# Batch 0 of a Fourier mixing kernel: load order, folds, and the E row of its first four steps

## The chip, the cores and the metric

The kernel runs on one core of a Trainium2 chip. The metric is device time in microseconds (us) of one launch. One run before the change was also recorded by the hardware profiler; all times of single instructions come from that run.

## The reference

`x` has 8 batches of 3008 rows and 256 columns. Each batch goes through a two-dimensional Fourier transform of which the real part is kept; the result, 24064 rows of 256, goes through a gated layer with d_ff = 1536.

```python
X = np.fft.fft(x, axis=1)          # along the 3008 rows
X = np.fft.fft(X, axis=2)          # along the 256 columns
x = X.real.astype(np.float32).reshape(B * S, D)
gate = 1.0 / (1.0 + np.exp(-(x @ w_gate)))
val = x @ w_val
return (gate * val @ w_out).astype(np.float32)
```

The three weights come from a float32 array multiplied by a numpy scalar, and reach the kernel as float64.

## The kernel before, in words

**The algebra.** The transform along the columns is linear, so it is merged into the weights: `merge` multiplies a block of 256 columns of w_gate or w_val by a small column table (`dt`) on TensorE and keeps two forms, G1 and G2. The transform along the rows is a multiplication by cosine and sine tables, made small by symmetry: rows s, 3008 - s, 1504 + s and 1504 - s are added and subtracted first (the folds), so that 126 partitions times 6 rows remain, and even and odd frequencies are summed apart. Each batch has three results over its 1505 frequencies: pk (cosine sums of the even column part, 128 partitions), qk (sine sums of the odd part, 128 partitions), and ek, the cosine sums of column 128 alone. ek is a single row of 1505 numbers; it is needed on all 128 partitions, since line 447 multiplies it by a scalar of each partition (`ge`, row 0 of G2 turned into a column by a small DMA).

**The main loop.** A step (`front`, `gate`, `back`) handles 256 frequencies and 128 columns of d_ff, for gate and value at once: TensorE makes pa = G1 · pk and pb = G2 · qk, VectorE makes ae = ek * ge + pa (line 447, twice), then z = ae + pb and ae - pb (lines 450 and 451), ScalarE takes the sigmoid, VectorE multiplies gate by value (line 462), GpSimd prepares differences, and TensorE multiplies by w_out (`back`). 12 steps make a chunk of 256 frequencies, 6 chunks a batch, 8 batches the kernel. PSUM for pa, pb and merges is a ring of four banks (`bank`); `po0` to `po3` are four more.

**The order is written by hand.** Each engine runs its instructions in program order. A dictionary `side` holds work to be issued at the end of a given step, `pre` work to be issued before the sigmoid of a step. SP issues nearly all DMAs, in program order; ScalarE's queue issues a few.

**The weights.** There are 18 blocks (`jobs`): gate c, value c and output c for c = 0 to 5. A float64 block is 512 KB. `weight_load` fetches it as pairs of int32; `weight_parts` is two ScalarE instructions (lines 221 and 222), `weight_join` three on VectorE (lines 231, 232, 234) and one addition on GpSimd (line 236). `weight_use` then merges the block (gate, value) or arranges it (`forms`, output). `weight_round` does parts and join of several blocks. Lines 252 and 253 copy G2 and G1 out of PSUM on ScalarE, line 255 issues the ge DMAs. In steps 0 to 8 the loop still prepares blocks 9 to 17.

**Batch 0 before the loop.** SP loads gate 0 and value 0, then x (two halves, line 116), the cosine table (two halves, line 159), four more blocks, the sine table, and four more. Gate 0 and value 0 are prepared and merged first. `fold_ops(0, 3)` folds x on VectorE with a share on GpSimd. TensorE makes the sums of pk and of ek (`cos`), each with 12 matmuls of 376 or 377 columns, ek with column 128 repeated 128 times as the stationary operand so that it comes out on all partitions; then the sine sums (`sin`). `places` (lines 370 and 373) puts sums and differences of even and odd parts into pk, qk, ek. For batches 1 to 7, `e_sums` makes ek of all seven at once, as rows of seven, stores them to DRAM (`ed`), and `seq_start` reads one row back to 128 partitions.

Of the kernel before, what the change touches and what calls it, by code (L numbers as in the profile page):

```python
# [7 lines left out]
F32 = mybir.dt.float32  # L8
# [43 lines left out]
def kernel(  # L52
# [101 lines left out]
    tr = dram.tile([P, 2, NQ, NE + NO], F32, name="tr")  # L154
    ed = dram.tile([B - 1, NK], F32, name="ed")

    def load_table(t, nq):
        for q in range(0, NQ, nq):
            nc.sync.dma_start(out=ST[0][0:NP, t, q : q + nq], in_=stab[:, t, q : q + nq])

# [15 lines left out]
    shared = {}  # L176
    KEEP = 10

    def weight_load(j):


        w, c = jobs[j]
        src = (moe_w_gate, moe_w_val, moe_w_out)[w]
        src = src[2 * c * P : 2 * (c + 1) * P, :] if w == 2 else src[:, c * WC : (c + 1) * WC]
        src = src.rearrange("(c p) f -> p c f", p=P)

        def some(n, pool, tag):

            key = tag, (j - 6) // 3 if tag == "c7" else 0
            if key not in shared:  # L190
                shared[key] = pool.tile([P, n, 2 * WC], F32, name=f"w{tag}", tag=tag)
            return shared[key]

        if j < KEEP:
            pool, tag = ((zp, "z"), (pqp, ("pk", "qk", "ek")[j % 3]), (op, "os"), (sp, "sf"))[
                j // 3 if j < 6 else j // 2 - 1]
            raw = pool.tile([P, 2, WC, 2], I32, name="raw", tag=tag)
            if j < 6:
                pool, tag = ((app, "ae"), (hp, "h"))[j // 3]
                ws = pool.tile([P, 2, WC], F32, name="ws", tag=tag)  # L200
            else:
                ws = some(3, cp, "c7")[:, (j - 6) % 3].rearrange("p (c f) -> p c f", c=2)
        else:
            both = some(12, xp, "x4")
            r, i = (j - KEEP) % 3 * 2, 6 + (j - KEEP) % 6
            raw = both[:, r : r + 2].rearrange("p a n -> p (a n)").bitcast(I32).rearrange(
                "p (c f w) -> p c f w", c=2, w=2)
            ws = both[:, i].rearrange("p (c f) -> p c f", c=2)
        WS[j] = ws
        if src.dtype == F32:  # L210
            nc.sync.dma_start(out=ws, in_=src)
        else:
            RAW[j] = raw
            nc.sync.dma_start(out=raw.rearrange("p c f w -> p c (f w)"), in_=src.bitcast(I32))

    def weight_parts(j):

        if j in RAW:
            raw, ws = RAW[j], WS[j]
            lo, hi = raw[:, :, :, 0], raw[:, :, :, 1]  # L220
            nc.scalar.activation(ws, hi.bitcast(F32), AF.Abs)
            nc.scalar.activation(lo, lo.bitcast(U32), AF.Copy, scale=2.0 ** -29)
# [22 lines left out]
    def merge(ws, g, c, other):  # L245
        cs = slice(c * WC, (c + 1) * WC)
        ps = bank("ps", other)
        for h in range(2):
            for t in range(2):
                mm(ps[:, h * WC : (h + 1) * WC], dt[:, t, h * HD : (h + 1) * HD], ws[:, t, :],  # L250
                   h == 0 and t == 0, t == 1)
        nc.scalar.copy(G2[:, g, cs], ps[:, WC : 2 * WC])
        nc.scalar.copy(G1[:, g, cs], ps[:, 0:WC])
        for f in range(c * WC // P, (c + 1) * WC // P):
            (nc.sync if c else nc.scalar).dma_start(
                out=ge[:, g, f : f + 1], in_=G2[0:1, g, f * P : (f + 1) * P])
# [16 lines left out]
    def fold_ops(b, nq):  # L273
# [18 lines left out]
        def across(e, blk, q):  # L292
            e.tensor_tensor(x4[:, 1 - blk, q], x4[:, 0, q], x4[:, 2, q],
                            op=(ALU.add, ALU.subtract)[blk])
# [19 lines left out]
        else:  # L314

            def half1(q):
                point(nc.vector, 2, 3, q)
                first(nc.vector, 2, 3, q)
                for blk in range(2):
                    across(nc.vector, blk, q)  # L320
                    feat(nc.vector, *parts[blk], q)

            def half2(q):
                across(nc.vector, 0, q)
                feat(nc.vector, *parts[0], q)
                across(pool, 1, q)
                feat(pool, *parts[1], q)
            for q in qs:
                point(nc.vector, 0, 1, q)
            first(nc.vector, 0, 1, slice(0, NQ))  # L330
            point(pool, 2, 3, qs[1])
            first(pool, 2, 3, qs[1])
            ops += [lambda: half1(qs[0]), lambda: half2(qs[1])]
        for blk, (v, r) in enumerate(parts):
            W[b, blk] = (v[:, :, 0:HD], r[:, :, 0:HD],
                         v[:, :, HD : HD + 1].to_broadcast([v.shape[0], NQ, P]))
        return ops
# [43 lines left out]
    def seq_start(b):  # L381
# [3 lines left out]
        if b:  # L385
            nc.sync.dma_start(out=PQE[b][2], in_=ed[b - 1 : b, :].to_broadcast([P, NK]))

# [13 lines left out]

    def e_sums():


        ps = bank("pe")
        m = B - 1
        at_ = lambda blk, par: slice((2 * blk + par) * TB, (2 * blk + par) * TB + m)
        for q in range(0, NQ, 2):
            for blk in range(2):
                c0, n = ((0, NE), (NE, NO))[blk]  # L410
                for par in range(2):
                    mm(ps[at_(blk, par), 0:n], x8[:, :, 1 + 2 * blk, q + par],
                       ST[0][0:NP, 0, q + par, c0 : c0 + n], q == 0, q == NQ - 2)
        er = cp.tile([P, NK], F32, name="er", tag="c7")[0:m]
        a = evp.tile([P, NE], F32, name="a", tag="a")[0:m]
        e1 = evp.tile([P, NE], F32, name="a", tag="a")[0:m]
        nc.scalar.copy(a, ps[at_(0, 1), 0:NE])
        nc.scalar.copy(e1[:, 0:NO], ps[at_(1, 0), 0:NO])

        def rest():  # L420
            places(er, 0, True, a, ps[at_(0, 0), 0:NE])
            nc.scalar.copy(a[:, 0:NO], ps[at_(1, 1), 0:NO])
            places(er, 1, False, e1[:, 0:NO], a[:, 0:NO])
            nc.scalar.dma_start(out=ed, in_=er)
        return rest

# [5 lines left out]
    def front(p, fh):  # L432
# [6 lines left out]
        pa = bank("pa").rearrange("p (g n) -> p g n", g=2)[:, :, 0:n]  # L439
        pb = bank("pb").rearrange("p (g n) -> p g n", g=2)[:, :, 0:n]  # L440
        for g in range(2):
            mm(pa[:, g], G1[:, g, fs], pk[:, ks], g == 0, True)
        for g in range(2):
            mm(pb[:, g], G2[:, g, fs], qk[:, ks], g == 0, True)
        ae = app.tile([P, 2, CH], F32, name="ae", tag="ae")[:, :, 0:n]
        for g in range(2):
            nc.vector.scalar_tensor_tensor(out=ae[:, g], in0=ek[:, ks], scalar=ge[:, g, f : f + 1],  # L447
                                           in1=pa[:, g], op0=ALU.mult, op1=ALU.add)
        z = zp.tile([P, 2, 2, CH], F32, name="z", tag="z")[:, :, :, 0:n]
# [116 lines left out]
    nc.gpsimd.memset(zero, 0.0)  # L566
    nc.scalar.dma_start(out=dt, in_=dtab.rearrange("(c p) d -> p c d", p=P))
    for j in range(2):
        weight_load(j)
    load_x(0)  # L570
    load_table(0, NQ // 2)
    for j in range(2, 6):
        weight_load(j)
    load_table(1, NQ)
    for j in range(6, KEEP):
        weight_load(j)

    def weight_round(*js):
        for j in js:
            weight_parts(j)  # L580
            weight_join(j)

    weight_parts(0)
    weight_parts(1)
    weight_join(0)
    weight_join(1)
    weight_use(0)
    weight_use(1)
    seq_start(0)
    cos = [seq_group(0, blk, what, (2 * blk, 2 * blk + 1) if what else None)  # L590
           for blk in range(2) for what in (0, 2)]
    for i, f in enumerate(fold_ops(0, NQ // 2)):
        f()
        for sums, _, _ in cos:
            sums(*range(i * NQ // 2, (i + 1) * NQ // 2))
    sin = [seq_group(0, blk, 1) for blk in range(2)]
    for sums, _, _ in sin:
        sums(*range(NQ))
    evacuate = [then for _, then, _ in cos + sin]
    for then, js in zip(evacuate, ((2, 3, 4), (5,), (), (), (6, 7), (8,))):  # L600
        weight_round(*js)
        then()()
    for j in range(KEEP, KEEP + 3):
        weight_load(j)
    weight_use(2)

# [12 lines left out]
    pre = {}  # L619
    for j in range(9, len(jobs)):  # L620
        pre.setdefault(j - 9, []).append(lambda j=j: weight_parts(j))
        at(j - 9, lambda j=j: weight_join(j))
        if KEEP <= j < len(jobs) - 3:
            at(j - 9, lambda j=j: weight_load(j + 3))
    for j in range(3, len(jobs)):
        w, c = jobs[j]
        at(2 * c + (-3, -2, 1)[w], lambda j=j: weight_use(j))

# [12 lines left out]
    at(3 * i0, e_fold)  # L641
    split(3 * i0 + 3, e_sums)
    at(3 * i0 + 5, table_again)
# [91 lines left out]
```

## Time and profile before

| | |
|---|---|
| three runs | 1992.41, 1993.08, 1996.01 us; median 1993.08 |
| profiled execution | span 1992.2 us, mean granted TensorE clock 0.996 |
| x halves have landed, by the waits of line 280 | 11.29 and 16.33 us |
| folds on VectorE end, last sine sum on TensorE ends | 26.7 and 49.7 us |
| first step starts (first pa matmul) | 51.24 us |
| the step with the last weight block ends | about 98 us |

The page gives busy time of each engine over the whole span; the timeline gives the instructions of one engine in order of time, with the idle time before each and what ended it. PE is TensorE, DVE VectorE, ACT ScalarE, POOL GpSimd, SP the engine that issues DMAs. Numbers after L are lines of the kernel. A float32 matmul stands as two records.

### The profile page before, as it was taken

The page shows a single profiled execution, that of the slowest core. Times are in us where ns is not written, and L with a number is a line of the kernel's source. Part 1 is how long each engine was busy: PE and PEld are TensorE (multiplying, and loading weights), DVE is VectorE, ACT ScalarE, POOL GpSimd, SP SyncE. Part 2 cuts the span into 40 slices and gives each one's busy share as a digit, 9 for nine tenths or more (in the row PEclk, how much of TensorE's full clock was granted, in tenths as well). Part 3 has the DMA queues.
Part 4 walks back from the last instruction along what each step waited for, and adds up shares of the span by engine and source line. Part 5 has one row for each costly group of instructions (what it writes and reads, how often), then busy time and mean ns, then how long its engine had stood idle before and what let it go on. Part 6 is the DMA issues. An engine that isn't in the chain of part 4 may idle for free.

```text
span 1992.2 us, 28166 instructions
## 1 busy us (share of the span) xinstructions
PE 1965.1 (99%) x9504; PEld 1737.3 (87%) x9504; DVE 1777.8 (89%) x3221; ACT 497.2 (25%) x876; POOL 1348.3 (68%) x1704
## 2 busy tenths in 40 slices
PE   6999999999999999999999999999999999999998
PEld 4888889888988889888898888988899888998888
DVE  7999979978999789997999979999799988898887
ACT  3422222222222222222222222222222222222221
POOL 3678867865787467874678646886478854655655
PEclk8999999999999999999999999999999999999999
DMA  7262421112020201202011020111200000000001
GB/s 265 85 134 77 154 90 48 48 27 75 16 66 25 82 19 23 73 11 90 17 44 46 17 90 17 43 47 32 75 11 12 21 27 11 11 20 12 11 17 26
DMA packets 160815, 100.33 MB, mean 50 GB/s; under 512 B 128419, under 2 KB 151715, under 8 KB 157994
## 3 DMA queue, kind: packets, MB, share of 16 engines
q1 hardware_dynamic: 158850, 98.00, 17.0%
q8 instruction: 76, 1.25, 0.3%
q10 hardware_dynamic: 1822, 0.54, 0.1%
q14 instruction: 67, 0.55, 0.1%
HBM read 73.74 MB, written 50.17 MB: 62 GB/s over the span
## 4 chain that ended last, share of the span: by engine, by line
PE 96%; DMA 2%; DVE 1%; ACT 0%; issue 0%; POOL 0%; SPq 0%; ACTq 0%; DVEq 0%; POOLq 0%
PE po L100 43%; PE pa L100 24%; PE pb L100 24%; PE ev L100 4%; DMA ge<-G 1%; DMA st<-in_stab_dram 1%; PE od L100 1%; PE ps L100 0%; DMA raw<-in_moe_w_val_dram 0%; DVE ae L447 0%; POOL wx L236 0%; PE pe L100 0%; DVE z L451 0%; DVE wx L232 0%; DVE os L509 0%
## 5 line engine op out<-in xcount | busy, mean ns | idle before, releaser
L672 ACT ACTIVATE z<-z 128x512 f32<-128x512 f32 (+1 forms) x576 | 358.5, 622 | 1297.5 <-DVE z L451 1297.5
L100 PE MATMUL pb<-qk,G 128*128 128x256 f32 (+1 forms) x2304 | 581.8, 375 | 2.5 <-DVE ae L447 2.5
L100 PE MATMUL pa<-pk,G 128*128 128x256 f32 (+1 forms) x2304 | 582.1, 375 | 0.0
L447 DVE SCALAR_TENSOR_TENSOR ae<-ek,ge,pa 128x256 f32<-128x256 f32 (+1 forms) x1152 | 488.1, 464 | 68.5 <-PE pa L100 65.0
L100 PE MATMUL po<-sf,wf 128*128 128x256 f32 (+1 forms) x2304 | 534.6, 375 | 0.0
L466 POOL TENSOR_TENSOR sf<-h 128x256 f32<-128x256 f32 (+1 forms) x288 | 206.9, 718 | 448.7 <-DVE h L462 448.7
L100 PEld LDWEIGHTS pb<-qk,G 128*128 128x128 f32 x2304 | 437.3, 190 | 53.6 <-DVE ae L447 4.0
L100 PEld LDWEIGHTS pa<-pk,G 128*128 128x128 f32 x2304 | 437.1, 190 | 51.7 <-issue 2.3
L100 PEld LDWEIGHTS po<-sf,wf 128*128 128x128 f32 x2304 | 437.7, 190 | 49.8 <-POOL sf L468 0.3
L462 DVE TENSOR_TENSOR h<-z 128x512 f32<-128x512 f32 (+1 forms) x576 | 480.6, 834 | 0.0
L450 DVE TENSOR_TENSOR z<-ae,pb 128x512 f32<-128x512 f32 (+1 forms) x576 | 390.1, 677 | 61.4 <-DVE ae L447 1.4
L100 PE MATMUL po<-h,wf 128*128 128x256 f32 (+1 forms) x1728 | 412.5, 375 | 0.0
L451 DVE TENSOR_TENSOR z<-ae,pb 128x512 f32<-128x512 f32 (+1 forms) x576 | 386.3, 671 | 0.0
L100 PEld LDWEIGHTS po<-h,wf 128*128 128x128 f32 x1728 | 328.3, 190 | 37.1
L464 POOL TENSOR_TENSOR sf<-h 128x256 f32<-128x256 f32 (+1 forms) x288 | 206.8, 718 | 96.4 <-DVE h L462 95.5
L468 POOL TENSOR_TENSOR sf<-h,sf 128x256 f32<-128x256 f32 (+1 forms) x288 | 207.8, 721 | 22.6
L467 POOL TENSOR_TENSOR sf<-sf,h 128x256 f32<-128x256 f32 (+1 forms) x288 | 207.7, 721 | 22.6
L100 PE MATMUL ev<-st,x 63*128 63x376 f32 (+4 forms) x372 | 98.5, 417 | 7.9 <-DVE x L290 5.9
L100 PEld LDWEIGHTS ev<-st,x 63*128 63x128 f32 (+1 forms) x372 | 66.5, 187 | 35.5 <-DVE x L290 6.3
L100 PE MATMUL od<-st,x 63*128 63x376 f32 (+4 forms) x372 | 97.4, 413 | 0.0
L549 ACT COPY c<-po 128x512 f32<-128x512 f32 (+1 forms) x141 | 75.5, 580 | 39.4 <-PE po L100 38.9
L509 DVE STREAM_TRANSPOSE os<-c 128x256 f32<-128x256 f32 x192 | 83.8, 436 | 0.2
(91 smaller groups left out, 830.2 us busy)
## 6 DMA issues: line engine op xcount, KB each, us to landing
x<-xr SPq DMA_DIRECT2D x14, 1536.0 KB
out_dram<-os SPq DMA_DIRECT2D x288, 64.0 KB
xr<-in_xf_dram SPq DMA_DIRECT2D x14, 768.0 KB
xr<-in_xf_dram SPq DMA_DIRECT2D x35, 256.0 KB
ek<-ed SPq DMA_DIRECT2D x7, 752.5 KB
out_dram<-os SPq DMA_DIRECT2D x92, 56.0 KB
x<-in_xf_dram SPq DMA_DIRECT2D x2, 1512.0 KB
tr<-in_stab_dram SPq DMA_DIRECT2D x2, 1129.5 KB
```

Of the source, the lines that this page charges most:

```text
L100: nc.tensor.matmul(o, l, r, start=start, stop=stop, skip_group_check=True)
L447: nc.vector.scalar_tensor_tensor(out=ae[:, g], in0=ek[:, ks], scalar=ge[:, g, f : f + 1], in1=pa[:, g], op0=ALU.mult, op1=ALU.add)
L450: nc.vector.tensor_tensor(z[:, :, 0], ae, pb, op=ALU.add)
L451: nc.vector.tensor_tensor(z[:, :, 1, ::-1], ae, pb, op=ALU.subtract)
L462: nc.vector.tensor_tensor(h[:, fh], z[:, 0], z[:, 1], op=ALU.mult)
L464: tt(s[:, 2], h[:, 0, 0], h[:, 0, 1], op=ALU.subtract)
L466: tt(s[:, 0], h[:, 0, 1], h[:, 1, 1], op=ALU.add)
L467: tt(s[:, 1], s[:, 0], h[:, 0, 0], op=ALU.subtract)
L468: tt(s[:, 3], h[:, 1, 0], s[:, 1], op=ALU.subtract)
L509: nc.vector.transpose(os_[:, s, 0:nb, h, :], t[:, slot, 0 : nb * TB])
L549: nc.scalar.copy(t[:, 2 * j : 2 * j + 2, 0:n], PO[j][:, :, 0:n])
L672: nc.scalar.activation(z[:, 0], z[:, 0], AF.Sigmoid)
```

## The change

Only work ahead of the twelfth step is touched. In the order of the program:

- **Loads.** x and the cosine table come first, then the first half of the sine table, gate 0 and value 0, the second half of the sine table, and blocks 2 to 11 (KEEP is 12 instead of 10). The raw blocks lie in other buffers, and the place of a converted block is taken when it is converted (`weight_place`).
- **Folds** of batch 0 run on VectorE alone.
- **E.** The ek sums of batch 0 are made by the same function as those of the other batches: a stationary operand of one column, in four column tiles of one PSUM bank (po3). The row is written to partition 0 of ek and stored to row 0 of `ed` (now 8 rows) by ScalarE's queue; from there one DMA of ScalarE's queue, issued last before the loop, brings it to the other 127 partitions.
- **The first four steps** (ROWS) add E on TensorE, with two matmuls of one partition into pa, and ScalarE copies pa to ae. From step 4 on line 447 does it as before.
- **Order.** Cosine sums, E and sine sums are all made before the first merges; blocks 0 to 6 are converted between their evacuations, merges of gate 0 and value 0 follow the sine sums. In the loop blocks 7 to 17 are converted in steps 0 to 10; gate c is merged at the end of step 2c - 2 and value c at the end of step 2c - 1 (before: 2c - 3 and 2c - 2).
- **ge.** All ge DMAs are issued by SP; those of gate 0 and value 0 were on ScalarE's queue.

```diff
@@ weight_load, weight_place
-    KEEP = 10
+    KEEP = 12
+    ROWS = 4
...
+            pool, tag = (((zp, "z"), (hp, "h"))[j // 3] if j < 6 else (sp, "sf") if j == 6 else
+                         (pqp, ("pk", "qk", "ek")[j - 7]) if j < 10 else (op, "os"))
...
+    def weight_place(j):
+
+        if j < 3:
+            return app.tile([P, 2, WC], F32, name="ws", tag="ae")
+        if j < 9:
+            ws = some(3, cp, "c7", j // 3)[:, j % 3]
         else:
+            ws = some(12, xp, "x4", 0)[:, 6 + (j - 9) % 6]
+        return ws.rearrange("p (c f) -> p c f", c=2)
@@ merge
         for f in range(c * WC // P, (c + 1) * WC // P):
-            (nc.sync if c else nc.scalar).dma_start(
+            nc.sync.dma_start(
                 out=ge[:, g, f : f + 1], in_=G2[0:1, g, f * P : (f + 1) * P])
@@ fold_ops, batch 0
-            def half1(q):
+            def rest(q):
                 point(nc.vector, 2, 3, q)
                 first(nc.vector, 2, 3, q)
                 for blk in range(2):
                     across(nc.vector, blk, q)
                     feat(nc.vector, *parts[blk], q)
-
-            def half2(q):
-                across(nc.vector, 0, q)
-                feat(nc.vector, *parts[0], q)
-                across(pool, 1, q)
-                feat(pool, *parts[1], q)
             for q in qs:
                 point(nc.vector, 0, 1, q)
             first(nc.vector, 0, 1, slice(0, NQ))
-            point(pool, 2, 3, qs[1])
-            first(pool, 2, 3, qs[1])
-            ops += [lambda: half1(qs[0]), lambda: half2(qs[1])]
+            ops += [lambda q=q: rest(q) for q in qs]
@@ e_sums, now for any number of rows m
+        def sums(*qs):
+            for q, p in zip([q for q in qs if q % 2 == 0] + [NQ] * len(qs),
+                            [q for q in qs if q % 2] + [NQ] * len(qs)):
+                for blk in range(2):
+                    c0, n = ((0, NE), (NE, NO))[blk]
+                    for par, r in enumerate((q, p)):
+                        if r < NQ:
+                            mm(ps[at_(blk, par), 0:n], col(blk, r), st[0:NP, 0, r, c0 : c0 + n],
+                               r < 2, r >= NQ - 2)
...
+                nc.scalar.dma_start(out=ed[b : b + m], in_=er)
@@ front
+        rows = 2 * p + fh < ROWS
         for g in range(2):
-            mm(pa[:, g], G1[:, g, fs], pk[:, ks], g == 0, True)
+            mm(pa[:, g], G1[:, g, fs], pk[:, ks], g == 0, not rows)
...
+        if rows:
+            for g in range(2):
+                mm(pa[:, g], G2[0:1, g, fs], ek[0:1, ks], False, True)
+            nc.scalar.copy(ae, pa)
+        else:
+            for g in range(2):
+                nc.vector.scalar_tensor_tensor(out=ae[:, g], in0=ek[:, ks],
+                                               scalar=ge[:, g, f : f + 1], in1=pa[:, g],
+                                               op0=ALU.mult, op1=ALU.add)
@@ ahead of the loop
-    for j in range(2):
-        weight_load(j)
     load_x(0)
-    load_table(0, NQ // 2)
-    for j in range(2, 6):
-        weight_load(j)
-    load_table(1, NQ)
-    for j in range(6, KEEP):
+    for q in range(0, NQ, N3):
+        load_table(0, q)
+    load_table(1, 0)
+    for j in range(2):
+        weight_load(j)
+    load_table(1, N3)
+    for j in range(2, KEEP):
         weight_load(j)
...
+    halves = range(N3), range(N3, NQ)
     seq_start(0)
-    cos = [seq_group(0, blk, what, (2 * blk, 2 * blk + 1) if what else None)
-           for blk in range(2) for what in (0, 2)]
+    cos = [seq_group(0, blk, 0) for blk in range(2)]
+    cos.append(e_sums(lambda blk, q: W[0, blk][2][:, q, :], 1, 0, PQE[0][2][0:1], 3) + (None,))
...
+    sin = [seq_group(0, blk, 1, (2 * blk, 2 * blk + 1)) for blk in range(2)]
+    for qs in halves:
+        for sums, _, _ in sin:
+            sums(*qs)
+    for (_, then, _), js in zip(cos + sin, ((0,), (), (1, 2), (3, 4), (5, 6))):
+        then()()
         weight_round(*js)
-        then()()
+    for j in range(2):
+        weight_use(j)
     for j in range(KEEP, KEEP + 3):
         weight_load(j)
-    weight_use(2)
+    nc.scalar.dma_start(out=PQE[0][2][1:P], in_=ed[0:1, :].to_broadcast([P - 1, NK]))
@@ in the loop
-    for j in range(9, len(jobs)):
-        pre.setdefault(j - 9, []).append(lambda j=j: weight_parts(j))
-        at(j - 9, lambda j=j: weight_join(j))
+    for i, j in enumerate(range(7, len(jobs))):
+        pre.setdefault(i, []).append(lambda j=j: weight_parts(j))
+        at(i, lambda j=j: weight_join(j))
...
-        at(2 * c + (-3, -2, 1)[w], lambda j=j: weight_use(j))
+        at((2 * c - 2, 2 * c - 1, max(2 * c + 1, j - 6))[w], lambda j=j: weight_use(j))
```

## The prediction

> **What bounds the kernel now.** I read the page first, then the timeline of each engine over the first 112 us, because the diff touches nothing after the twelfth step of the main loop. From the page:
>
> ```profile
> PE 1965.1 (99%) x9504; PEld 1737.3 (87%) x9504; DVE 1777.8 (89%) x3221; ACT 497.2 (25%) x876; POOL 1348.3 (68%) x1704
> ...
> PE 96%; DMA 2%; DVE 1%; ACT 0%; issue 0%; POOL 0%; SPq 0%; ACTq 0%; DVEq 0%; POOLq 0%
> ```
>
> TensorE is idle for 27 us of 1992.2, and the chain that ended last lies 96% on it. So a shift of the moment from which TensorE runs without a break passes to the end one for one. Its timeline shows the start:
>
> ```profile
> 9.31 6.01 PE L100 MATMUL ps<-ws,dt 128*128 128x256 f32 x16 [9.31 <-POOL ws L236]
> 21.19 2.88 PE L100 MATMUL ev<-st,x 126*128 126x377 f32 x4 [5.87 <-DVE x L290]
> ...
> 40.15 3.00 PE L100 MATMUL ev<-st,x 126*128 126x377 f32 x6 [2.02 <-DMA st<-in_stab_dram]
> ...
> 51.24 1.03 PE L100 MATMUL pa<-pk,G 128*128 128x256 f32 x4
> ...
> 73.38 1.13 PE L100 MATMUL pb<-qk,G 128*128 128x256 f32 x4 [1.49 <-DVE ae L447]
> ```
>
> Columns: start, busy, and in brackets the idle time before and who ended it. The first step begins at 51.24; one matmul is two records. The steps after it wait for VectorE, whose timeline says why:
>
> ```profile
> 29.66 0.42 DVE L231 TENSOR_SCALAR ws<-ws 128x512 f32<-128x512 f32 x1
> 30.12 1.39 DVE L232 TENSOR_SCALAR ws<-ws 128x512 int32<-128x512 int32 x1
> 31.55 0.69 DVE L234 SCALAR_TENSOR_TENSOR ws<-raw,ws 128x512 int32<-128x512 int32 x1
> ...
> 53.28 0.69 DVE L450 TENSOR_TENSOR z<-ae,pb 128x512 f32<-128x512 f32 x1
> ...
> 72.84 0.48 DVE L447 SCALAR_TENSOR_TENSOR ae<-ek,ge,pa 128x256 f32<-128x256 f32 x1 [1.30 <-DMA ge<-G]
> ```
>
> The first three lines are one conversion of a weight block (a "join"): 1.55 us of work, 2.4 us when the GpSimd addition of the block before (1.3 us) overlaps it. A step with a join takes VectorE 5.05 us: line 447 of step 4 to that of step 9 runs from 72.84 to 98.07. TensorE works 4.97 us in such a step (pa and pb 1.73, back 1.5, merge 1.73). **Until the last join both engines are full, and VectorE leads.** At 106.15, where pa of step 13 starts, TensorE runs without waits.
>
> The third reading is of DMA: the windows view (TensorE clock, DMA share, GB/s at the end), then the DMA view of 171.5 to 174.5, where one table mirror is under way.
>
> ```profile
> 8.00:13.00 5.00, 3.69 (x9) 2.97 (x10) 3.91 (x5) 0.23 (x1) 2.54 (x2) 1.00 0.87 359
> ```
>
> ```profile
> DMA packets 62, 0.14 MB, mean 47 GB/s; under 512 B 2, under 2 KB 28, under 8 KB 62
> ...
> q1 hardware_dynamic: 62, 0.14, 12.7%
> ...
> tr<-in_stab_dram SPq DMA_DIRECT2D x1, 188.0 KB
> ```
>
> From 8 to 13 us only x (126 rows) moves: 0.87 of 16 engines is 14. The mirror has two planes outermost: 12.7% is two engines, 23 GB/s each. So the rows decide how many engines work.
>
> **What the Trainium skill says.** "DMA: Bandwidth & Descriptors", section "Why a DMA increments its semaphore by 16 and not by 1": the engine count is the largest divisor up to 16 of the slowest dimension; 127 partitions go to one engine. The two windows above agree (14 for 126, 2 for 2); 127 itself is not in this trace. Same page, "Queues, rings and completion order": each engine alternates between queues packet by packet. The trace agrees: a ge transfer on ScalarE's queue took 10.19 us (14.12 to 24.31, chain view) beside a full SP queue, and 2.96 us at 73.58. "TensorEngine Tiling (Array Packing)", "When to Use Tiling": narrow stationary operands share the array; in e_sums 24 records of 0.48 us take 2.02 us (193.87 to 195.89). "TensorE: Matmul & The Clock Gate", Part 1: an idle array falls to half clock; at 21.19 four records take 2.88 us, later 1.43.
>
> **The change, part by part** (times are estimates from the rows named).
>
> *Loads.* Two weight blocks (1.05 MB at 328 GB/s, 3.2 us) no longer precede x. Its halves landed at 11.29 and 16.33 (line 280's waits), now about 8.1 and 12.5. At 350 GB/s: cosine halves 16.2 and 20, first sine half 24, blocks 0 and 1 by 26, second sine half 30, blocks 2 to 6 by 37 (1.3 us each).
>
> *Folds.* GpSimd's share moves to VectorE: 1.05 us (line 280) and 2.05 us (lines 293, 287, 288, 290). A half takes 5.2 us on VectorE, and the 1.8 to 2 us stretches beside GpSimd (17.20, 24.69) go. Folds end at 12.5 + 10.4 = 22.9; now at 28.7 on GpSimd.
>
> *Sums.* Twelve ek matmuls (0.634 us each, 7.6 us) become column tiles, 2 us with two mode changes. TensorE from 16.2: 24 matmuls 15.2, E 2.0, cold start 2.5: sums end at 36, now 49.5. Merges 0 and 1 (3.5 us) follow.
>
> *ScalarE.* E's sums end at 28.5; two copies, four one-row places (0.54 us, as wide as before) and block 0's join make er ready at 32.2. The store of E waits for that on ScalarE's queue; blocks 1 and 2 are queued behind. Then six blocks (1.2 us), two copies (0.45) and four G copies (0.27) make 9.2 us: first step at about 41.5, **broadcast issued at 42.0.** Its wait for the stored row (2 to 3 us) is hidden by those 9 us; ae of step 0 is behind it.
>
> *VectorE.* From 33.4: joins 1 to 6 (13 us) and the sine places (2.0): z of step 0 at 48.4, against 53.28. Of 10 us that TensorE gains, 5 are left, because the joins did not shrink.
>
> *Steps 0 to 3.* Out: two of line 447 each (0.87 us on VectorE). In: a 0.58 us ScalarE copy and two one-row matmuls, streaming 256 columns as pa does (0.43 each): 0.86 us of TensorE per step, 3.5 in all. They lie beside VectorE's z 1.3, h 0.6 and join 2 to 2.4. Merges now stand right before the step that needs them, so pa of an even step waits for sigmoid and copy. Bounds per step: 3.9 (VectorE's work alone) and 5.05 (as with line 447 now). I take 4.4; line 447 of step 4, with its ge, could run at 48.4 + 4 × 4.4 = 66.
>
> *At nothing.* KEEP 12 loads two more blocks early; they land behind all others, by 44, and are joined from step 3 on (past 60). One more merge lies in the loop (ten for nine, 1.73 us of TensorE): VectorE leads there. The raw blocks' new places (z, h, sf, os) are free once joined, before z or h of the same buffer is written.
>
> *The broadcast.* Row E goes to 127 partitions, 1505 floats each: 764 KB. On all 16 engines the 128-row form (ek<-ed) needs about 4 us. On one engine: 764 KB / 26 GB/s (359 over 14) = 29.3 us. The SP queue alternates with it: four ge transfers move there from ScalarE's queue, ahead of blocks 12 to 14, then ge of each merge. About 56 packets of 2 KB on that engine (84 ns at 24 GB/s) and 100 tiny ones: 6.6 us. Bounds: 29.3 (nothing shared) to 40 (each packet slowed as the mirror's, and an SP transfer reusing the semaphore). I take 36: 42.8 + 36 + 0.7 lands at 79.5. Line 447 of step 4 waits until 80; behind it on VectorE stand z of step 4, h of 3, join 11; TensorE stops at pb of step 5. ge, queued on the same engine, comes in the same time.
>
> *The rest.* Steps 4 to 10 each have a join (seven where before had five left after step 4): 7 × 5.05 = 35.3. In steps 6, 8, 10 ge has no spare step: its 2 to 3 us exceed the join beside it by about 1.2, three times 3.6 (bounds 0 and 6). Line 447 of step 11 ends at 80 + 35.3 + 3.6 + 0.9 = 119.8, and pa of step 13 follows; before 106.15. **Sum: +13.7 us**, 2005.9 on this profile's span. The median of the runs is 0.9 above that span: **2006.8**. Cold clock after the stall: 0 to 2 us, taken as 0 since VectorE leads there.
>
> **Rivals.** (1) *Not slower: the broadcast spreads.* Its place is step 4, its price the 14 us from 66 to 80; it vanishes once the transfer takes under 23 us, as two engines would manage. Then 66 + 35.3 + 3.6 + 0.9 = 105.8 against 106.15: TensorE's gain is eaten by the same joins, 1992.7. For: the 128-row form lands in 4 us. Against: 126 rows used 14 engines. (2) *Faster: it spreads and the joins run at 1.55 us with ge hidden.* Saves 3.6 and about 3: 1986. Against: the joins at 29 to 34 us run at 2.4. (3) *Step 0's one-row matmuls wait for the whole ek tile, not row 0.* Then the first step starts at 79.5 and line 447 of step 4 at 79.5 + 4 × 4.4 = 97, 17 us after the forecast's 80: 2024. Against: x is already used by halves.
>
> **How the numbers follow.** Forecast 0.84, rival 1 0.08, rival 2 0.05, rival 3 0.03. The forecast's own range: landing 71 (issue at 40, nothing shared), ge hidden: 1995; landing at 84, cold clock, ge at its worst: 2014. That leaves out the rivals, 0.16, and 0.04 of its tails. About 0.2% (4 us) can be told from no change here. Slower: 0.84 less 0.04 that end under 1997, plus rival 3: 0.83; same 0.10; faster 0.07.
>
> **What would show it.** Right: line 447 of step 4 waiting over 10 us for DMA ek near 80; a stretch near 50 to 78 with ek's queue at about one sixteenth; sums over at 36; z of step 0 near 48. Wrong: ek landed by 50, or no stall at step 4; then rivals 1 and 2 are told apart by z of step 10 (102 or 97; before 102.21).

## The result, and the profile after

The changed kernel takes 2030.07 us (median of 4 runs, 2027.73 to 2030.49) against 1993.05 (also 4 runs, 1992.41 to 1996.01): a ratio of 1.018, with a 95% interval of [1.0163, 1.0198]. Its profiled span is 2025.6 against 1992.2, 33.4 us more. The direction was forecast, the size was not: 2006.8 was the forecast, 2014 its upper end.

The page of the kernel after, the lines of engines and of the chain that ended last:

```profile
PE 1973.6 (97%) x9520; PEld 1738.5 (86%) x9520; DVE 1771.4 (87%) x3219; ACT 499.4 (25%) x881; POOL 1340.2 (66%) x1698
...
PE 93%; DMA 4%; DVE 1%; ACT 1%; issue 0%; POOL 0%; SPq 0%; ACTq 0%; DVEq 0%; POOLq 0%
PE po L100 41%; PE pa L100 24%; PE pb L100 24%; PE ev L100 4%; DMA ek<-ed 2%; DMA raw<-in_moe_w_out_dram 1%; DMA st<-in_stab_dram 1%; DMA ge<-G 1%; PE od L100 0%; DVE ae L460 0%; DVE z L465 0%; POOL wx L239 0%; DVE wx L235 0%; DVE z L464 0%; PE ps L100 0%
```

TensorE was idle for 27 us, now for 52; the other 8.5 us of the 33.4 are more busy time (1973.6 against 1965.1), some of it at half clock, as is shown further down. DMA has 4% of the chain instead of 2%, and the broadcast (ek<-ed) alone has 2%. Old line 447 is now 460, 450 is 464, and 255 (ge) is 258; in the experiments they can stand some lines further down.

TensorE's timeline of the kernel after, to be held against the one of before:

```profile
19.14 2.85 PE L100 MATMUL ev<-st,x 126*128 126x377 f32 x4 [19.14 <-DMA st<-in_stab_dram]
...
48.64 1.25 PE L100 MATMUL pa<-pk,G 128*128 128x256 f32 x4 [2.45 <-ACT G L256]
51.06 2.07 PE L100 MATMUL pb<-qk,G 128*128 128x256 f32 x4 [1.18 <-DVE qk L364]
...
55.07 3.78 PE L100 MATMUL ps<-ws,dt 128*128 128x256 f32 x8
...
88.26 2.07 PE L100 MATMUL pb<-qk,G 128*128 128x256 f32 x4 [6.07 <-DVE ae L460]
...
124.51 3.02 PE L100 MATMUL ps<-wx,dt 128*128 128x256 f32 x8 [3.30 <-POOL wx L239]
...
138.82 0.70 PE L100 MATMUL po<-h,wf 128*128 128x256 f32 x2 [1.44 <-POOL wf L265]
```

The first step starts 2.6 us earlier than before (48.64 against 51.24), not 10. By z of step 0 that is lost too (55.85 against 53.28). Then comes step 4's wait at 88.26, and more behind it. VectorE's timeline of the same kernel shows whom TensorE waits for:

```profile
9.31 1.82 DVE L283 TENSOR_TENSOR x<-x 126x765 f32<-126x765 f32 x2 [9.31 <-DMA x<-in_xf_dram]
15.52 0.96 DVE L283 TENSOR_TENSOR x<-x 126x765 f32<-126x765 f32 x1 [4.31 <-DMA x<-in_xf_dram]
...
41.04 0.43 DVE L234 TENSOR_SCALAR ws<-ws 128x512 f32<-128x512 f32 x1 [5.19 <-ACT ws L224]
...
55.85 0.69 DVE L464 TENSOR_TENSOR z<-ae,pb 128x512 f32<-128x512 f32 x1
...
63.21 0.69 DVE L464 TENSOR_TENSOR z<-ae,pb 128x512 f32<-128x512 f32 x1 [4.38 <-ACT ae L457]
...
86.47 0.48 DVE L460 SCALAR_TENSOR_TENSOR ae<-ek,ge,pa 128x256 f32<-128x256 f32 x1 [8.50 <-DMA ge<-G]
87.73 0.48 DVE L460 SCALAR_TENSOR_TENSOR ae<-ek,ge,pa 128x256 f32<-128x256 f32 x1 [0.77 <-DMA ge<-G]
...
102.79 0.48 DVE L460 SCALAR_TENSOR_TENSOR ae<-ek,ge,pa 128x256 f32<-128x256 f32 x1 [5.15 <-DMA ge<-G]
...
113.19 0.48 DVE L460 SCALAR_TENSOR_TENSOR ae<-ek,ge,pa 128x256 f32<-128x256 f32 x1 [0.88 <-DMA ge<-G]
117.81 0.48 DVE L460 SCALAR_TENSOR_TENSOR ae<-ek,ge,pa 128x256 f32<-128x256 f32 x1 [4.14 <-DMA ge<-G]
...
129.22 0.48 DVE L460 SCALAR_TENSOR_TENSOR ae<-ek,ge,pa 128x256 f32<-128x256 f32 x1 [1.88 <-PE pa L100]
```

Step 4 waits 8.5 us and 0.8 more, steps 6 and 8 another 5 us each, and always the wait that ends last is for ge, not for ek. Line 460 of step 10 alone waits for TensorE. The chain of waits, followed back from 135 us, tells why (start, duration, what):

```profile
46.29 36.82 DMA ek<-ed
83.69 0.60 SPq L258
84.39 0.55 SPq L258
84.98 0.60 SPq L258
85.68 2.02 DMA ge<-G
87.73 0.49 DVE ae L460
...
97.38 1.28 POOL wx L239
99.16 3.60 DMA ge<-G
102.79 0.49 DVE ae L460
```

The broadcast lasts 36.82 us and ends at 83.12. Only then does SP issue the six ge transfers that come next in its order, from 83.18 on and about 0.6 us apart; step 4 needs the third and the fifth of them. At step 6 the order is different: GpSimd's addition frees a raw buffer, SP issues the block load that waited for it, then ge, and VectorE waits for that ge. SP's own waits, 55 to 125 us (total, times, longest):

```profile
SPq L258 <- DMA ek<-ed: 22.7, 1, 22.7
SPq L258 <- ACT G L256: 12.7, 3, 5.2
...
SPq L200 <- POOL wx L239: 9.1, 1, 9.1
```

SP, which has nothing to do with the broadcast, stands 22.7 us for its end. A semaphore is the counter by which a DMA tells that it has landed. In the trace, successive DMAs of the program take eight semaphores in turn, whatever queue they are on, and each issue waits until the DMA that had its semaphore before has landed. The third ge of the loop takes the semaphore of the broadcast, and goes out at 83.18. The first two were issued at 59.28 and 59.80, and landed only at 80.30 and 82.43. The DMA view of 62 to 80 us, where little else moves:

```profile
DMA packets 123, 0.47 MB, mean 26 GB/s; under 512 B 13, under 2 KB 13, under 8 KB 122
...
q10 hardware_dynamic: 61, 0.37, 4.9%
q1 hardware_dynamic: 61, 0.10, 1.5%
```

q10 is ScalarE's queue, q1 is SP's. Together they fill 6.4% of 16 engines: one engine, which takes one packet of each queue in turn (61 of each). SP's packets are the shares of its own loads on this engine: blocks 12 to 14, issued at 50.96 to 52.04, landed at 67.77, 72.98 and 78.17.

### The profile page after: what moved, and what is told of

It is laid out like the page before. It is cut to its first block, busy times and chain, and to the rows that moved or that the text cites. A ratio compares the mean times of both kernels' runs of the same rounds, so it can differ in the third digit from the quotient of the medians.

```text
span 2025.6 us, 28184 instructions
## 1 busy us (share of the span) xinstructions
PE 1973.6 (97%) x9520; PEld 1738.5 (86%) x9520; DVE 1771.4 (87%) x3219; ACT 499.4 (25%) x881; POOL 1340.2 (66%) x1698
## 4 chain that ended last, share of the span: by engine, by line
PE 93%; DMA 4%; DVE 1%; ACT 1%; issue 0%; POOL 0%; SPq 0%; ACTq 0%; DVEq 0%; POOLq 0%
PE po L100 41%; PE pa L100 24%; PE pb L100 24%; PE ev L100 4%; DMA ek<-ed 2%; DMA raw<-in_moe_w_out_dram 1%; DMA st<-in_stab_dram 1%; DMA ge<-G 1%; PE od L100 0%; DVE ae L460 0%; DVE z L465 0%; POOL wx L239 0%; DVE wx L235 0%; DVE z L464 0%; PE ps L100 0%
## 5 line engine op out<-in xcount | busy, mean ns | idle before, releaser
L100 PE MATMUL ev<-st,x 63*128 63x376 f32 (+4 forms) x360 | 93.8, 413 | 19.3 <-DMA st<-in_stab_dram 19.1
L100 PE MATMUL od<-st,x 63*128 63x376 f32 (+3 forms) x360 | 92.8, 410 | 0.0
```

Source lines behind the costliest of these rows:

```text
L100: nc.tensor.matmul(o, l, r, start=start, stop=stop, skip_group_check=True)
```

## The experiments

All runs (ratio to the kernel before, each against runs of it on the same chip; starts of z of steps 0, 4 and 12 and of pa of step 13 in the profiled run):

| run | median us | ratio [95%] | span | z 0 | z 4 | z 12 | pa 13 |
|---|---|---|---|---|---|---|---|
| before | 1993.05 | 1 | 1992.2 | 53.3 | 73.4 | 108.1 | 106.2 |
| after | 2030.07 | 1.018 [1.0163, 1.0198] | 2025.6 | 55.8 | 88.3 | 138.4 | 139.4 |
| r1_spread | 2019.28 | 1.0114 [1.0092, 1.0136] | 2017.2 | 57.3 | 78.8 | 130.2 | 131.2 |
| r2_gefirst | 2020.11 | 1.012 [1.0098, 1.0142] | 2018.2 | 57.6 | 90.4 | 131.0 | 132.0 |
| r3_spread_gefirst | 2008.50 | 1.0066 [1.004, 1.0091] | 2005.4 | 55.7 | 77.2 | 118.4 | 119.4 |
| r4_slack | 2020.67 | 1.0119 [1.0095, 1.0144] | 2017.7 | 58.8 | 76.9 | 130.6 | 131.6 |
| r5_store | 2005.32 | 1.005 [1.0035, 1.0065] | 2000.3 | 52.7 | 72.5 | 113.3 | 114.3 |
| r6_rows0 | 2006.87 | 1.0058 [1.0043, 1.0073] | 2004.9 | 57.8 | 77.1 | 117.9 | 118.9 |
| r7_store_rows0 | 2007.55 | 1.0062 [1.0047, 1.0078] | 2005.7 | 59.2 | 78.0 | 118.7 | 119.6 |
| r8_ge_act | 2018.28 | 1.012 [1.0103, 1.0137] | 2015.5 | 53.7 | 73.7 | 128.5 | 129.5 |
| r9_sp | 1999.22 | 1.0026 [1.0016, 1.0036] | 1996.8 | 50.3 | 68.7 | 109.8 | 110.7 |
| r10_sp_folds | 2000.33 | 1.003 [1.0018, 1.0043] | 1998.3 | 52.0 | 70.4 | 111.2 | 112.2 |
| r11_sp_spare | 2000.78 | 1.0034 [1.0022, 1.0047] | 2000.4 | 53.1 | 71.2 | 113.4 | 114.3 |
| r12_both | 2002.05 | 1.0039 [1.0026, 1.0052] | 1998.9 | 51.9 | 70.0 | 111.9 | 112.9 |
| r13_store_only | 2028.15 | 1.0164 [1.0149, 1.0178] | 2026.0 | 50.8 | 87.8 | 138.9 | 139.8 |
| r14_blocks_first | 2002.34 | 1.0038 [1.0023, 1.0052] | 1998.8 | 51.8 | 71.1 | 111.8 | 112.7 |
| r15_blocks_first_spare | 2001.28 | 1.0024 [1.0014, 1.0034] | 2001.1 | 58.1 | 77.8 | 115.7 | 115.1 |

In every row pa of step 13 is later than before by what the span is longer, within 0.2 us, so the whole loss lies ahead of that step. The kernel before took 1993.84 to 1995.87 (medians) in its runs beside the experiments; medians of different rows can therefore be off against each other by 2 us, and the ratios are the surer figures.

**The two suspects, alone and together.** r1_spread cuts the broadcast into 112 and 15 rows; r2_gefirst issues ge ahead of the block load in each step.

```diff
@@ r1_spread
-    nc.scalar.dma_start(out=PQE[0][2][1:P], in_=ed[0:1, :].to_broadcast([P - 1, NK]))
+    for p0, p1 in ((1, 113), (113, P)):
+        nc.scalar.dma_start(out=PQE[0][2][p0:p1], in_=ed[0:1, :].to_broadcast([p1 - p0, NK]))
@@ r2_gefirst
-        if KEEP <= j < len(jobs) - 3:
-            at(i, lambda j=j: weight_load(j + 3))
...
         at((2 * c - 2, 2 * c - 1, max(2 * c + 1, j - 6))[w], lambda j=j: weight_use(j))
+    for i, j in enumerate(range(7, len(jobs))):
+        if KEEP <= j < len(jobs) - 3:
+            at(i, lambda j=j: weight_load(j + 3))
```

> The broadcast of E goes out as two transfers of 112 and 15 rows, so that 16 and 15 engines work instead of one; nothing else differs from the changed kernel. Theory A (the single engine is the main cause of the 37 us, through its own 37 us, the ge transfers that share its engine, and the SP queue that waits for its semaphore): step 4 finds ek and ge in time and the kernel falls to 2005 us or below. Theory B (most of the loss lies in merges that have lost their spare step, with ge queued on SP behind the load of a weight block): only the 9.3 us that line 460 of step 4 waited come back, about 2021 us; the waits of 5.2 and 4.1 us in steps 6 and 8 stay.

> Within each step of the loop SP issues the ge transfers ahead of the load of the next weight block; the broadcast stays on one engine. Theory A: no difference, 2030 us, since ge was late because of the broadcast. Theory B: the waits for ge in steps 6 and 8 (5.2 and 4.1 us) fall to about 1 us each, 2022 us; step 4 still waits for the broadcast.

> Both edits, the broadcast on 16 and 15 engines and ge ahead of the loads. Theory A: as the first of these runs, 2005 us or below. Theory B: the two gains add, about 2012 us. My forecast's own sum for a kernel without the broadcast's stall was 1993 us; if steps 0 to 3 are as slow here as in the changed kernel (5 to 10 us each instead of 4.4) it stays 15 to 20 us above that.

The cut broadcast brings 10.8 us (2030.07 to 2019.28), ge first 10.0, both 21.6: they add up, as Theory B said, so they are two losses. From z of step 0 to that of step 12 the gains are 9.6, 9.1 and 19.8. VectorE's timeline of r1_spread has no wait at step 4 any more, but the later ones unchanged:

```profile
93.65 0.48 DVE L460 SCALAR_TENSOR_TENSOR ae<-ek,ge,pa 128x256 f32<-128x256 f32 x1 [5.11 <-DMA ge<-G]
...
108.83 0.48 DVE L460 SCALAR_TENSOR_TENSOR ae<-ek,ge,pa 128x256 f32<-128x256 f32 x1 [4.25 <-DMA ge<-G]
```

In r2_gefirst it is the other way round:

```profile
88.59 0.48 DVE L460 SCALAR_TENSOR_TENSOR ae<-ek,ge,pa 128x256 f32<-128x256 f32 x1 [9.14 <-DMA ge<-G]
...
100.02 0.48 DVE L460 SCALAR_TENSOR_TENSOR ae<-ek,ge,pa 128x256 f32<-128x256 f32 x1 [0.28 <-DMA ge<-G]
```

**A spare step for every merge.** r4_slack is r3_spread_gefirst with all merges of gate and value blocks one step earlier, as in the kernel before.

```diff
@@ r4_slack
-    for j in range(2):
+    for j in range(3):
         weight_use(j)
...
-        at((2 * c - 2, 2 * c - 1, max(2 * c + 1, j - 6))[w], lambda j=j: weight_use(j))
+        at((2 * c - 3, 2 * c - 2, max(2 * c + 1, j - 6))[w], lambda j=j: weight_use(j))
```

> As the run before, and gate 1 is merged ahead of the loop and every gate and value block one step earlier, as in the kernel before the change. Theory B: pa of an even step no longer waits for the copy of G (8.7 us in all in the changed kernel) and ge has a step to spare: 8 to 10 us less than the run before, about 2003 us. Theory A: no difference to the run before.

A miss: 12 us slower than r3_spread_gefirst. Steps 0 to 3 gain (18.1 us from z 0 to z 4 instead of 21.5), the later ones lose more: 53.7 us from z 4 to z 12. SP's waits, 55 to 100 us, then those of all engines, 60 to 125 us:

```profile
SPq L258 <- ACT G L256: 28.7, 7, 6.7
```

```profile
PE ps L100 <- POOL wx L239: 12.5, 3, 4.8
```

I took the first line for the cause: SP waits for merges and so issues block loads late. r8_ge_act tests it, with ge on ScalarE's queue (and with r5_store's edit, below).

> r4_slack (merges one step early, broadcast in 112 and 15 rows), with the store of row E behind blocks 3 and 4, and with ge issued on ScalarE's queue, so that SP's block loads wait behind nothing. Theory D1 (r4_slack lost because SP, in order, held the block loads behind ge; a spare step alone is worth some 5 us in steps 0 to 3 and some 8 later): 1996 to 2000. Theory D2 (ScalarE, waiting at each ge issue for its merge or for a semaphore, holds conversions and copies in SP's place): 2004 to 2012.

Both ranges were missed (2018.28), and TensorE again waits 12.7 us for GpSimd's additions. (In such waits the clock falls too: r4_slack has PEclk 0.50 from 98.8 to 105.5 us.) So the second line is the likelier cause: seven blocks instead of nine are joined ahead of the loop, block j in step j - 7 instead of j - 9. Merged one step earlier, blocks 14 and 15 are merged in the very step that joins them, and block 11 one step behind. That is too close too: TensorE's program runs a step ahead of VectorE's here. r11_sp_spare below, which leaves blocks 14 and 15 where they were, loses 1.6 us against its own base and not 12. The missing spare step is not a choice of the change; its later joins force it.

**Steps 0 to 3.** r5_store issues the store of row E behind the conversions of blocks 3 and 4; r6_rows0 takes away the one-row matmuls (ROWS = 0); r7_store_rows0 does both; r9_sp is r5_store with the broadcast on SP's queue.

```diff
@@ r5_store
-                nc.scalar.dma_start(out=ed[b : b + m], in_=er)
+                if b:
+                    nc.scalar.dma_start(out=ed[b : b + m], in_=er)
...
         weight_round(*js)
+        if 4 in js:
+            nc.scalar.dma_start(out=ed[0:1], in_=PQE[0][2][0:1])
@@ r9_sp
-        nc.scalar.dma_start(out=PQE[0][2][p0:p1], in_=ed[0:1, :].to_broadcast([p1 - p0, NK]))
+        nc.sync.dma_start(out=PQE[0][2][p0:p1], in_=ed[0:1, :].to_broadcast([p1 - p0, NK]))
```

> As r3_spread_gefirst, and the store of row E waits on ScalarE's queue behind the conversions of blocks 3 and 4 instead of ahead of those of blocks 1 and 2. Theory B1 (the store's wait for an earlier load's landing stops ScalarE and so VectorE's joins, and this passes on): VectorE's 5 us of idle time from 36 to 41 is gone, z of step 0 starts at 50.5 to 51.5 instead of 55.7, every later step shifts along, and the time is 2003 to 2004.5. Theory B2 (what limits steps 0 to 3 is something else, so that z of step 0 coming early is lost by step 4): z of step 4 within 1.5 us of r3's 77.2 and 2007 to 2009.

> As r3_spread_gefirst, with line 460 used from step 0 on: no one-row matmuls, no copy of ae by ScalarE, the broadcast row waited for by step 0. Theory C1 (the one-row matmuls and ScalarE's copy, which stands behind the conversions in ScalarE's order, make steps 0 to 3 slow: z waits 7.3 us for it): steps 0 to 3 take 5.05 us each as before, 20.2 instead of 21.5 from z of step 0 to z of step 4, but z of step 0 itself waits for the broadcast and for ge (landing 53 to 55), so 2006 to 2009. Theory C2 (the steps are slow because merges stand right ahead of the steps that use them): no gain in steps 1 and 2, 2009 to 2012.

> r5_store and r6_rows0 together. The row's later store puts the broadcast and ge later, but joins run on: if line 460 in steps 0 to 3 costs nothing there, the same as r5_store within 2 us; if the early TensorE addition of E is worth its copies, slower than r5_store by 3 to 5 us.

> r5_store with both parts of the broadcast issued by SP, behind the first loads, instead of ScalarE, which in r5 stood 8.7 us at the second part (from 42.95 to 51.66) until a block load landed that has the same semaphore. Theory E1 (ScalarE's wait holds the copy of ae and so z of step 0): z of step 0 at 50 instead of 52.7, some 2.5 us off all later steps, span 1997 to 1998.5. Theory E2 (VectorE is full until 50 anyway, and the chain z, sigmoid, copy of G, pa, one-row matmuls, copy of ae takes over in step 1): under 1 us, span 1999.5 to 2001.

r5_store: VectorE's stop before 41.04 is gone, and the span is 5.1 us shorter (2005.4 to 2000.3), z 4 earlier by 4.7: B1, but z 0 came at 52.7, later than expected, and the intervals of the two ratios overlap (1.005 and 1.0066). ScalarE's timeline of r5_store shows the rest:

```profile
51.66 0.33 ACTq L620 DMA_DIRECT2D ek<-ed  x1
52.09 0.58 ACT L458 COPY ae<-pa 128x512 f32<-128x512 f32 x1 [8.71 <-DMA raw<-in_moe_w_gate_dram]
```

The second part of the broadcast takes the semaphore of block 11's load, which landed at 51.64; ScalarE stands from 43.4 until then. On SP's queue (r9_sp) this holds nobody, and 3.5 us of span are gained: E1. The one-row matmuls alone are worth nothing measurable as long as the store's wait delays step 0 (r6_rows0 against r3_spread_gefirst); with the store mended, z 4 comes 5.5 us earlier with them (72.5 against 78.0), though the intervals of the times still overlap.

**What of the rest.** r9_sp is still 5 us slower than before. r10_sp_folds shares the folds with GpSimd again; r11_sp_spare moves only the merges of blocks 2 to 12 a step earlier, with ge behind the loads; r12_both does both. r14_blocks_first loads and joins gate 0 and value 0 ahead of x; r15_blocks_first_spare joins an eighth block ahead of the loop too and gives every merge a spare step.

```diff
@@ r11_sp_spare
+        s = int(c < 5)
+        at((2 * c - 2 - s, 2 * c - 1 - s, max(2 * c + 1, j - 6))[w], lambda j=j: weight_use(j))
@@ r14_blocks_first
+    for j in range(2):
+        weight_load(j)
     load_x(0)
...
+    weight_round(0, 1)
     halves = range(N3), range(N3, NQ)
```

> r9_sp with the folds of x shared with GpSimd as in the kernel before. Theory F1 (VectorE leads from 35 to 50 and every join moves forward by what GpSimd takes): 2 to 3 us faster than r9_sp. Theory F2 (x is waited for until 15.5; GpSimd then ends its share near 28, 2 us later than VectorE alone, TensorE's sums end at 41 to 42 instead of 39, and VectorE, which only waits for the sums from 25 to 28, gains nothing): the same as r9_sp or up to 2 us slower.

> r9_sp with the merges of blocks 2 to 12 one step earlier, those of 14 and 15 left where they are (their blocks are joined only in the step before), and ge behind the block loads in each step as in the changed kernel. Theory G1 (merges right ahead of the step that uses them cost steps 0 to 3 some 0.6 to 1 us each, by a chain through sigmoid and the copy of G; r4 and r8 lost only because blocks 14 and 15 were merged in the step that joins them): 2 to 4 us faster than r9_sp, near 1994 to 1997. Theory G2 (the spare step is no gain because VectorE leads in every step): the same as r9_sp within 1 us, or slower where a merge makes TensorE wait for a join.

> r10_sp_folds and r11_sp_spare together: the sum of their two differences from r9_sp within 1.5 us if each stands on its own; if both act on the same time of VectorE, only the larger one. Under 1993 only if F1 and G1 both hold.

> r9_sp with weight blocks 0 and 1 loaded ahead of x, as in the kernel before, and joined before the folds; nothing else changed, seven blocks are joined ahead of the loop as in r9_sp. Theory J1 (VectorE is full from 35 to step 10 and idles only while x is on its way, so two joins there are worth 2 x 2.4 and the later x costs 3.2): z of step 0 1 to 2 us earlier than in r9_sp, 1997 to 1998.5. Theory J2 (TensorE's sums, 3 us later, take over): z of step 0 at 52 to 53, 2000 to 2002.

> r14_blocks_first with eight blocks joined ahead of the loop instead of seven, ten left for it, and every merge one step earlier, which leaves each merge a step behind its join and a spare step ahead of its use. Theory K1 (the loop's loss is one of missing slack: merges right behind joins or right ahead of uses): no wait of DVE for ge or of TensorE for GpSimd's addition over 1 us, steps of 5.05 from step 4 on and one step with a join less: z of step 12 at 107 to 109, 1994 to 1997. Theory K2 (the eighth join ahead of the loop moves z of step 0 back by as much as it saves later): the same as r14_blocks_first within 1.5 us.

None gains. r10 and r14 end about as F2 and J2 said, r11 as the second half of G2 (1.6 us slower), r15 as K2; r12_both loses 2.8, the sum of r10's 1.1 and r11's 1.6. In r14 the two joins stand where VectorE was idle, but x and its sums come later, and z 0 moves from 50.3 to 51.8. r11_sp_spare's first steps are a little shorter (18.1 us to z 4 instead of 18.4), but z 0 comes 2.8 us later, and what the steps gain goes ahead of step 6, at the merge of block 11 one step behind its join (TensorE's timeline):

```profile
78.11 2.62 PE L100 MATMUL ps<-wx,dt 128*128 128x256 f32 x8 [3.36 <-POOL wx L239]
```

r15 shows both sides: 37.9 us from z 4 to z 12 instead of 41.1, and z 0 at 58.1 instead of 50.3. No version here beats the kernel before.

**Was the front hidden?** r13_store_only is the changed kernel with r5_store's edit alone.

> The changed kernel with nothing but the store of row E moved behind the conversions of blocks 3 and 4. Theory H1 (the wait delays the issue of the broadcast, which lasts 36.8 us whatever stands beside it, and step 4 waits for its end): issued at 42.7 instead of 46.3, landed at 79.5 instead of 83.1, 3 to 4 us faster than the changed kernel, 2026 to 2027. Theory H2 (hidden): 2029 to 2031.

```profile
85.97 0.48 DVE L461 SCALAR_TENSOR_TENSOR ae<-ek,ge,pa 128x256 f32<-128x256 f32 x1 [16.27 <-DMA ge<-G]
```

z 0 starts 5 us earlier, step 4 waits 16.27 us instead of 8.50, and z 4 comes at 87.8 instead of 88.3: hidden, as H2 said. The time itself, 2028.15, lies between the two ranges and decides nothing. The broadcast was issued at 43.72 and landed at 82.61, in 38.9 us instead of 36.8. Started earlier, it probably found more of the block loads' packets on its engine; this was not measured.

## Why the prediction was right, and where it was wrong

- **The broadcast: right.** "On one engine", 36 us: 36.82 measured, at one sixteenth of 16 engines, and the stall at step 4 is there. The Trainium skill's rule ("DMA: Bandwidth & Descriptors", "Why a DMA increments its semaphore by 16 and not by 1") holds for 127 rows, which went to one engine; in r3_spread_gefirst 112 rows took 4.6 us. The broadcast was issued at 46.29 and not at 42.0, and so landed 3.6 us later than the forecast's 79.5.
- **ge beside it: wrong.** "ge, queued on the same engine, comes in the same time" had line 447 of step 4 at 80. It ran at 87.73 for its second half: 3.6 us for the later landing, and 4.1 us more than assumed passed between landing and line 460. For the two ge that were out the sentence was right (80.30 and 82.43). The next ones were not slowed but not issued: SP was stopped by a semaphore that the broadcast held, and afterwards five of them had to go out one by one. The upper bound of 40 us for the transfer had "an SP transfer reusing the semaphore" in it, as a slower transfer and not as SP's queue standing with all that follows.
- **ge in the later steps: wrong, and the largest term.** The sum had ge's "2 to 3 us exceed the join beside it by about 1.2, three times 3.6 (bounds 0 and 6)". The 39.8 us from line 447 of step 4 to pa of step 13 came out as 51.6 (87.73 to 139.36), 11.8 more. Of these, 8.3 lie between z of step 4 and z of step 11: the steps that end with z of 6 and of 8 took 9.9 us each instead of 5.05, with waits for ge of 5.15, 0.88 and 4.14 in them, the one that ends with z of 10 took 1.9 more than 5.05, the others 0.3 together; that is 11.9 where the sum had 3.6. (The 5.05 was read from the second of step 4's two instructions to the first of step 9's; from z to z such a step takes 5.12 before, 73.42 to 99.03.) The sum priced ge's transfer and left out its place: SP works in order, and the block load ahead of ge waits for a GpSimd addition of the same step. r2_gefirst, which changes that order alone, gets 10 us back. The working's own question, what is queued behind a waiting instruction, was put to VectorE and not to SP.
- **"pa of step 13 follows": wrong.** Here lie the other 3.5 us of the 11.8. From z of step 11 to pa of step 13 it took 3.8 us (135.60 to 139.36), 1.44 of them TensorE's wait at 138.82 for GpSimd's part of the last but one output block, the rest matmuls.
- **"VectorE leads there": wrong at step 10.** On this ground one more merge in the loop and the cold clock stood at nothing. At 124.51 TensorE waited 3.30 us for the GpSimd addition with which the join of block 15 ends. The merge then took 3.02 us instead of 1.89 and pa of step 10 1.86 instead of 1.03, at half clock (the windows view has a granted clock of 0.50 from 125.4 to 128.7 us), and VectorE waited 1.88 us for it.
- **The first steps: wrong, without a cost here.** z of step 0 came at 55.85 instead of 48.4. The loads were reckoned at 350 GB/s; the windows view has 261 to 309 in its stretches from 8 to 13 and from 16 to 38 us. TensorE's sums began at 19.14 and not at 16.2, E took 2.8 us in two parts and not 2.0, and the sums ended at 39.8 and not at 36. x's second half was there at 15.52, not 12.5; blocks 2 to 6, "by 37", landed from 37.03 to 42.43. The store of E stopped ScalarE for 5.52 us, since it takes the semaphore of block 4's load, which landed only at 39.73.

  Steps 0 to 2 took 6.1 us each (to 74.15) instead of 4.4: 7.4, 5.9 and 5.1. The first of them ran at half clock. The windows view has the granted clock in the third place from the end, and it was 0.50 throughout from 50.3 to 60.4 us:

```profile
46.00:54.00 8.00, 4.37 (x11) 2.59 (x11) 7.76 (x14) 3.13 (x8) 3.64 (x4) 0.76 0.49 155
54.00:62.00 8.00, 8.00 (x22) 5.74 (x21) 4.72 (x7) 4.27 (x7) 3.49 (x3) 0.60 0.44 154
```

  The merge at 55.07 took 3.78 us instead of 1.89, and VectorE waited 4.38 us at 63.21 for what comes behind it. r13_store_only shows the late start hidden behind step 4. Where nothing hides it and the clock stays full, r9_sp has 4.6 us per step, and its step 1 again 5.9. What sets this longer step is the chain that the forecast only named, "pa of an even step waits for sigmoid and copy". The chain of waits of r9_sp, and the line of TensorE's timeline:

```profile
54.66 0.63 ACT z L688
55.88 0.70 PE pa L100 x2
56.58 0.86 PE pb L100 x4
57.44 1.05 PE pa L100 x4
```

```profile
55.88 0.70 PE L100 MATMUL pa<-pk,G 128*128 128x256 f32 x2 [1.14 <-ACT G L256]
```

  G's copy stands behind the sigmoid on ScalarE, pa behind the copy, and the sum of E behind pa.
- **The sum.** 3.6 + 4.1 + 11.8 are, up to rounding, the 19.6 us by which pa of step 13 was late (139.36 against 119.8). It was 33.2 us later than before and the span is 33.4 longer, so "passes to the end one for one" was right. The runs' median lies 4.5 us above the profiled span and not 0.9 (the profiled run was the fastest of the four): 3.6 more. Together 23.2 of the 23.3 us missed.
- **The rivals.** Rival 1 said that a spread broadcast gives 1992.7. r1_spread has it and takes 2019.28, because its 105.8 has the same wrong terms for the first and the later steps; with the issue order, the store and the broadcast's queue mended too r9_sp takes 1999.22. Rival 3 (2024) has nearly the right time and the wrong reason: the first step started at 48.64, the one-row matmuls wait for row 0 alone.
- **Joins.** "TensorE's gain is eaten by the same joins" is borne out: in r9_sp z of step 4 starts 4.7 us earlier than before and that of step 10 still 0.3, but pa of step 13 comes 4.6 us later, which is all that its span is longer. TensorE's timeline of r9_sp shows where it goes:

```profile
96.91 2.00 PE L100 MATMUL ps<-wx,dt 128*128 128x256 f32 x8 [1.05 <-POOL wx L239]
...
110.21 0.70 PE L100 MATMUL po<-h,wf 128*128 128x256 f32 x2 [1.67 <-POOL wf L265]
```

  Joins end in step 10 instead of step 8. The merge of block 15 now lies between pa of steps 9 and 10 and waits for its join (6.5 us from pa to pa, before 3.45), and step 12 waits for GpSimd's part of an output block (4.95 us, before 3.02). From pa of step 9 to that of step 13 r9_sp needs 18.5 us, before it was 13.0. r15_blocks_first_spare, with one join less in the loop and its merges a step earlier, needs 12.95 there; but its z of step 0 comes 6.3 us later than in r14_blocks_first, and so it wins nothing.

## What to carry to other kernels

When a change lets a DMA become slow or a small one urgent, walk the issuing queue in order and ask of each entry what it waits for: a buffer, a producer, and the semaphore it inherits (here from the DMA eight before). Here a transfer of 127 rows cost its own 37 us and held up the transfer that came to share its semaphore, with all behind it; cut into 112 and 15 rows it was gone. And before moving work ahead of the loop, check whether the engine that will lead there (here VectorE, by its joins) gets less to do; if not, the earlier start can be lost again, as here by step 13.

## What the runs showed of the hardware that was not expected

- **Semaphores in turn.** In this program a DMA is held until the one that last had its semaphore, eight DMAs before on whatever queue, has landed. It is the issuing instruction that waits, and with it all that its engine has to do behind it. Seen three times to within 0.1 us: ge at 83.18 behind the broadcast (83.12), the store of E at 39.80 behind a load (39.73), r5_store's second part at 51.66 behind another (51.64).
- **x ahead of everything came no sooner.** The windows view of 8 to 13 us after, with the DMA share and GB/s at the end:

```profile
8.00:13.00 5.00, 0.00 (x0) 0.00 (x0) 1.90 (x3) 0.00 (x0) 0.00 (x0) 1.00 0.92 309
```

  Before, it was 0.87 and 359. Here other transfers are queued behind x: more engines are busy and fewer bytes move. x's second half, with two blocks less ahead of it, was there only 0.8 us earlier (15.52 against 16.33). Why the rate falls was not tried.
- **A stall cools TensorE.** At 51.06 and at 88.26, after waits, pb's four records take 2.07 us instead of 1.03. The Trainium skill ("TensorE: Matmul & The Clock Gate", Part 1) has half clock after an idle window of about 3.4 us. At 88.26, after a wait of 6.07 us, the trace agrees. Before 51.06 no single wait was that long (2.51, 2.45 and 1.18 us), but TensorE had worked only 3.2 of the last 9.4 us. At 88.26 VectorE led and nothing was lost by it; in steps 0 and 10 VectorE waited for the slow matmuls (4.38 and 1.88 us). r9_sp, without the long waits, has PEclk 1.00 from 43 to 111 us.
